# All seven scalings of the last attention pair directly behind its sums, and fewer weight passes in the two drain steps

## The chip, the core and the metric

The kernel runs on one core of a Trainium2 chip. The metric is the device time of one execution in microseconds (us). The core's engines run their own instruction streams and wait for each other through semaphores: TensorE (PE) does the matmuls, VectorE (DVE) and ScalarE (ACT) the elementwise work, SyncE (SP) issues most of the loads and stores.

## The reference

What must be computed is causal attention over 2 batches of 12 heads (448 positions, 64 wide), then two feed-forward layers over the 896 tokens (768 wide, 2048 hidden), all in float32:

```
scores = q @ k.T / 8, masked above the diagonal
attn   = exp(scores - max);  attn = attn / sum(attn)
x      = attn @ v, as 896 x 768
h = relu(x @ w1);  x = (h * h) @ w2
h = x @ w3;        out = (h - tanh(h)) @ w4
```

The weights arrive as float64 words, which the kernel turns into pairs of float32r tiles on the chip.

## The kernel before, in words

**Attention.** Two heads are worked on together as a pair; there are 12 pairs, and `body` runs a loop of 14 steps (`s` = 0 to 13). In step `s`, pair `s` gets its scores, maxima and exponentials (`exps`, L305, on ACT, which also sums each row), pair `p = s - 1` gets its reciprocals (`recips`, L309 and L310) and its scalings by them (`norms`, L317, seven blocks of 64 to 448 columns, numbered 0 to 6, on DVE), and pair `a = s - 2` is transposed (`transposes`, L323, four batches of four on PE), copied out of PSUM (`tcopy`, L329, on ACT) and multiplied with v (`pv`, L341). The result goes to the tiles x as a rounded half (`xhi`, L354, ACT) and a remainder (`xlo`, L358, DVE). The two last steps, 12 and 13, have no new pair: they are called the drains here. In step 12 the last pair (11) is scaled and pair 10 is transposed; in step 13 pair 11 is transposed.

**Early matmuls.** From step 8 on, `fill` puts matmuls of the first layer (batch 0, L370 to L372, three per k) between the attention's PE instructions. They share one PSUM bank, which `relus` (L387, L388, L380 on ACT) empties and whose low half `relu_lows` (L383, DVE) writes.

**Weights.** Each of 64 weight units u (128 x 768 words) is loaded into one of three buffers (`w_load`, L98, SP) and prepared in four passes on DVE: shift (L115), merge (L120), sign (L125) and split (L134 for odd u, L136 for even u). ACT does a scaling of the exponent words (`w_exp`, L105, before merge) and a cast of the word that sign made (L127, before split). The order on DVE is shift(u), split(u-1), merge(u), sign(u), shift(u+1), and so on. Split(u) frees the buffer, and asks for the load of unit u+3.

**What sets the order.** Each engine runs its instructions in the order in which the code issues them. A call of `one` takes the next pass if the budget of the step is above zero (and, for sign, a ring place is free); `pump` takes passes until it isn't. The budget of a drain is `SHARE_LAST`; a pass takes 470 or 870 from it. ACT's share of a pass is put on the list `act_late` and issued by the next `late`.

**After the attention** come the groups of the first layer (8 column blocks m by 2 batches b, 18 matmuls each), then 12 groups of the second (24 matmuls each), and the whole once more for the other half of the hidden columns; then the second feed-forward layer in the same way. Six groups (m = 0 to 5, batch 0) are done early; the first one behind the drains is m = 6, batch 0, with unit 6.

Of the kernel before, what the change touches and what calls it, by code (L numbers as in the profile page):

```python
# [27 lines left out]
NPAIR = B * NP  # L28
# [6 lines left out]


SHARE_PAIR = (800, 3300)
SHARE_LAST = 6000
SHARE_HIDDEN = (2400, 500)
SHARE_OUT = 4000  # L40

# [23 lines left out]
def body(ctx: ExitStack, tc: tile.TileContext, qT, kT, vL, w1, w2, w3, w4, out):  # L65
# [29 lines left out]
    def w_load(u):  # L95
        if u < NU:
            raws[u] = sb.tile([P, UC], I64, tag="raw", bufs=3, name=f"raw{u}")
            nc.sync.dma_start(out=raws[u], in_=units[u])  # L98
# [54 lines left out]
    def room():  # L153
        i = len(taken) - RING
        return i < 0 or taken[i] < freed[0]
# [10 lines left out]
    def late():  # L166
        while act_late:
            act_late.pop(0)()

    def one():  # L170

        if todo and budget[0] > 0 and (room() or not todo[0][3]):
            take()
            return True

    def take():
        f, cost, _, _ = todo.pop(0)
        f()
        budget[0] -= cost
# [6 lines left out]
    def pump():  # L186
        while one():
            pass
# [29 lines left out]
    def warm(count):  # L218
        o = ps.tile([P, 512], F32, tag="h", bufs=1, name="warm")[:, :S]
        for _ in range(count):  # L220
            nc.tensor.matmul(o, lhsT=ones[:, :P], rhs=ones, start=True, stop=True)
# [41 lines left out]
    def scores(n, t):  # L263
        q, k = qk[n]
        banks = []
        for z, cs in enumerate(step(n, t)):
            bank = ps.tile([P, 512], F32, tag="s", bufs=4, name=f"s{n}_{t}_{z}")
            banks.append(bank)
            for c in cs:
                sc[n, c] = bank[:, SOFF[c] : SOFF[c] + D * (c + 1)]  # L270
        for i in range(2):
            for z, cs in enumerate(step(n, t)):
                for c in cs[i : i + 1]:
                    for j in range(2):
                        r, e = slice(D * j, D * j + D), D * (j ^ z)
                        nc.tensor.matmul(sc[n, c][e : e + D], lhsT=q[r, D * c : D * c + D], rhs=k[r, : D * (c + 1)], start=(c == cs[0]), stop=False, skip_group_check=True)  # L276
        for z, cs in enumerate(step(n, t)):
            d = [SOFF[c] // D + c for c in cs]
            o = banks[z].rearrange("p (b k) -> p b k", k=D)[:, d[0] : d[-1] + 1 : max(d[-1] - d[0], 1)]
            for j in range(2):  # L280
                r, e = slice(D * j, D * j + D), D * (j ^ z)
                nc.tensor.matmul(o[e : e + D], lhsT=identb[r, r], rhs=maskb[r, : len(cs)], start=False, stop=True, skip_group_check=True)
        if t == 1:
            qk.pop(n)
            load_qk(n + 3)

    def blocks(n, t):
        return [c for cs in step(n, t) for c in cs]

    def maxes(n, t):  # L290
        if t == 0:
            stat[n] = sb.tile([P, 3, 8], F32, tag="stat", bufs=4, name=f"st{n}")
        st = stat[n]
        cs = blocks(n, t)
        for c in reversed(cs):
            nc.vector.tensor_reduce(out=st[:, 0, SI[c] : SI[c] + 1], in_=sc[n, c], axis=AX.X, op=ALU.max, negate=True)  # L296
        a, z = SI[cs[0]], SI[cs[-1]] + 1
        nc.vector.tensor_scalar_mul(out=st[:, 0, a:z], in0=st[:, 0, a:z], scalar1=0.125)  # L298

    def exps(n, cs):  # L300
        st = stat[n]
        for c in cs:
            w = D * (c + 1)
            i = SI[c]
            nc.scalar.activation(prob[n % 3][:, POFF[c] : POFF[c] + w], sc.pop((n, c)), AF.Exp, bias=st[:, 0, i : i + 1], scale=0.125, accum_out=st[:, 1, i : i + 1])  # L305

    def recips(n):
        st = stat[n]
        nc.vector.tensor_scalar_add(out=st[:, 1, :NQ], in0=st[:, 1, :NQ], scalar1=1e-9)  # L309
        nc.vector.reciprocal(out=st[:, 2, :NQ], in_=st[:, 1, :NQ])  # L310

    def norms(n, cs):
        st = stat[n]
        for c in cs:
            i = SI[c]
            p = prob[n % 3][:, POFF[c] : POFF[c] + D * (c + 1)]
            nc.vector.tensor_scalar_mul(out=p, in0=p, scalar1=st[:, 2, i : i + 1])  # L317

    def transposes(n, t):
        bank = tb[n, t] = ps.tile([P, 512], F32, tag="t", bufs=2, name=f"t{n}_{t}")  # L320
        for i, (kc, c) in enumerate(TBLK[4 * t : 4 * t + 4]):
            o = bank.rearrange("p (i j q) -> p i j q", j=2, q=D)[:, i, :: -1 if c in TURNED else 1]
            nc.tensor.transpose(o, prob[n % 3][:, POFF[c] + P * kc : POFF[c] + P * kc + P], ident)  # L323

    def tcopy(n, t):
        if t == 0:
            pt[n] = slot(3 + n % 2, [P, 16, P], F32, f"pt{n}")
        bank = tb.pop((n, t))
        nc.scalar.copy(out=pt[n][:, 4 * t : 4 * t + 4], in_=bank.rearrange("p (i q) -> p i q", q=P))  # L329

    def pv(n, kcs):
        b, hp = divmod(n, NP)
        if 0 in kcs:
            ob[n] = ps.tile([P, 512], F32, tag="o", bufs=1, name=f"o{n}")
        o = ob[n]
        for kc in kcs:
            r = P if kc < 3 else D
            m = NQ - 2 * kc
            for j in range(2):
                h = 2 * hp + j  # L340
                nc.tensor.matmul(  # L341
                    o[D * j : D * j + D, P * kc : S],
                    lhsT=vs[b][kc][:r, D * h : D * h + D],
                    rhs=pt[n][:r, TBASE[kc] : TBASE[kc] + m, D * j : D * j + D],
                    start=(kc == 0),
                    stop=(kc == 3),
                    skip_group_check=True,
                )
        if 3 in kcs:
            pt.pop(n)  # L350

    def xhi(n):
        b, hp = divmod(n, NP)
        nc.scalar.copy(out=x[hp][:, 0, b], in_=ob[n][:, :S])  # L354

    def xlo(n):
        b, hp = divmod(n, NP)
        nc.vector.tensor_sub(out=x[hp][:, 1, b], in0=ob.pop(n)[:, :S], in1=x[hp][:, 0, b])  # L358
# [117 lines left out]
    def fill(count):  # L476
        for _ in range(count):
            next(early_groups, None)

    def relus():  # L480
        while done:
            h, dst = done.pop(0)
            lows.append((dst, relu2(h, dst)))

    def relu_lows():
        while lows:
            lo_of(*lows.pop(0))
# [34 lines left out]
    for s in range(NPAIR + 2):  # L522
        p, a = s - 1, s - 2
        ss, sp, sa = s < NPAIR, 0 <= p < NPAIR, a >= 0
        f = s - 2 >= NP
        if ss:
            budget[0] = min(budget[0], 0) + (SHARE_PAIR[f] if s > 1 else 0)
            e0, e1 = blocks(s, 0)[::-1], blocks(s, 1)
        else:
            budget[0] = min(budget[0], 0) + SHARE_LAST  # L530
        if sp:
            exps(p, blocks(p, 1)[-1:])
        if ss:
            scores(s, 0)
        if sa:
            norms(a, (3, 5, 6))
        if a >= 1:
            xhi(a - 1)
        if f:
            relu_lows()  # L540
            one()
            fill(1)
        if sa:
            transposes(a, 0)
            tcopy(a, 0)
            transposes(a, 1)
            tcopy(a, 1)
        late()
        if f:
            fill(2)  # L550
        if ss:
            maxes(s, 0)
        if a >= 1:
            xlo(a - 1)
        if f:
            one()
        if ss:
            exps(s, e0[:2])
        if sp:
            recips(p)  # L560
            norms(p, (0, 1, 2))
        if f:
            one()
        if ss:
            scores(s, 1)
        if f:
            fill(1)
        if sa:
            transposes(a, 2)
            tcopy(a, 2)  # L570
            transposes(a, 3)
            tcopy(a, 3)
        if f:
            fill(2)
        late()
        if ss:
            exps(s, e0[2:])
            maxes(s, 1)
            exps(s, e1[:-1])
        if sp:  # L580
            norms(p, (4,))
        relus()
        one()
        if f:
            one()
        if sa:
            pv(a, range(4))
        if not ss:
            pump()
        late()  # L590
        if s == 1:
            warm(5)
        if s in (2, 3):
            w_load(s - 1)
        if s == 4:
            load_v(1)
# [58 lines left out]
```

## Time and profile before

| | before |
|---|---|
| median of 3 runs | 567.02 us |
| lowest of them | 565.03 us |
| profiled execution | 565.34 us |
| its span | 563.5 us |
| PE busy in the span | 551.8 us (98%) |
| DVE busy | 403.8 us (72%) |
| ACT busy | 337.1 us (60%) |
| granted TensorE clock, mean | 0.997 |

The span is the time from the first to the last instruction; 1.84 us of the profiled execution lie around it. A busy PE is one whose pipeline holds a matmul; the duration of one overlaps the next one's, so that start-to-start distances tell the rate. A granted clock of 1.00 is the higher of the two levels (2.4 GHz), 0.50 the lower (1.2 GHz).

### The profile page before, as it was taken

Reading aid. Unit: us, or ns where it says so; the run is one execution under the profiler, and the core shown is the slowest. Engines: PE = TensorE matmul, PEld = TensorE weight load, DVE = VectorE, ACT = ScalarE, POOL = GpSimd, SP = SyncE. Lnnn points to the kernel's source line nnn. Section 1 sums busy time; section 2 is a strip of 40 time slices with the busy share of each in tenths; the row PEclk is TensorE's granted clock in tenths of the full one; section 3 lists DMA queues with packets and bytes.
Section 4 is the critical chain, followed back from the end, with each engine's and each line's share of the span. In section 5 each row is a group of like instructions: output and inputs, shape, how many; then the busy total and the mean of one; then the engine's idle time right before and its main releaser. Section 6 shows DMA issues by size and latency. Waiting matters only on the chain.

```text
span 563.5 us, 8049 instructions
## 1 busy us (share of the span) xinstructions
PE 551.8 (98%) x3134; PEld 482.3 (86%) x3134; DVE 403.8 (72%) x727; ACT 337.1 (60%) x650; POOL 1.8 (0%) x11
## 2 busy tenths in 40 slices
PE   7999999899999999999999999999999999999997
PEld 3667776699999999999999999999999999999996
DVE  5999988658564447555749489998888499889611
ACT  4999888658543238666325278776565487864200
POOL 1000000000000000000000000000000000000000
PEclk9999999899999999999999999999999999999999
DMA  8643412415342324333223330110665311015211
GB/s 292 235 150 106 147 57 82 142 57 168 113 169 94 131 61 163 112 113 112 72 97 116 109 113 1 56 58 15 209 223 176 120 42 56 1 57 173 94 49 49
DMA packets 15525, 61.85 MB, mean 110 GB/s; under 512 B 1664, under 2 KB 6400, under 8 KB 15488
## 3 DMA queue, kind: packets, MB, share of 16 engines
q1 hardware_dynamic: 15200, 61.00, 32.3%
q8 instruction: 24, 0.39, 0.3%
q10 hardware_dynamic: 288, 0.34, 0.2%
q14 instruction: 13, 0.11, 0.1%
HBM read 58.59 MB, written 2.75 MB: 109 GB/s over the span
## 4 chain that ended last, share of the span: by engine, by line
PE 83%; DVE 11%; ACT 2%; DMA 2%; SPq 1%; issue 0%; DVEq 0%; ACTq 0%
PE o L370 14%; PE o L371 14%; PE o L372 14%; PE h L370 13%; PE h L371 13%; PE h L372 13%; DVE st L296 4%; DVE p L317 2%; DMA k<-kT 2%; PE t L323 1%; ACT p L305 1%; DVE raw L120 1%; DVE x L358 1%; PE o L341 1%; DVE w L136 1%; PE s L276 1%
## 5 line engine op out<-in xcount | busy, mean ns | idle before, releaser
L370 PE MATMUL o<-g,w 128*128 128x448 f32 x384 | 140.4, 366 | 0.0
L371 PE MATMUL o<-g,w 128*128 128x448 f32 x384 | 140.4, 366 | 0.0
L372 PE MATMUL o<-g,w 128*128 128x448 f32 x384 | 140.1, 365 | 0.0
L370 PEld LDWEIGHTS o<-g,w 128*128 128x128 f32 x384 | 72.1, 188 | 6.0
L372 PEld LDWEIGHTS o<-g,w 128*128 128x128 f32 x384 | 72.1, 188 | 6.0
L371 PEld LDWEIGHTS o<-g,w 128*128 128x128 f32 x384 | 72.1, 188 | 5.8
L127 ACT CAST w<-raw 128x768 fp32r<-128x768 f32 x64 | 58.3, 911 | 30.6 <-DVE raw L125 30.6
L370 PE MATMUL h<-x,w 128*128 128x448 f32 x192 | 73.2, 381 | 2.4 <-ACT r L387 2.4
L105 ACT ACTIVATE raw<-raw 128x768 f32<-128x768 f32 x64 | 59.4, 928 | 24.4 <-DMA raw<-w 24.4
L371 PE MATMUL h<-x,w 128*128 128x448 f32 x192 | 70.8, 369 | 0.0
L372 PE MATMUL h<-x,w 128*128 128x448 f32 x192 | 70.7, 368 | 0.0
L372 PE MATMUL h<-y,w 128*128 128x448 f32 x192 | 70.6, 368 | 0.0
L371 PE MATMUL h<-y,w 128*128 128x448 f32 x192 | 70.6, 367 | 0.0
L370 PE MATMUL h<-y,w 128*128 128x448 f32 x192 | 70.6, 367 | 0.0
L125 DVE SCALAR_TENSOR_TENSOR raw<-raw 128x768 int32<-128x768 int32 x64 | 61.2, 957 | 1.2
L120 DVE SCALAR_TENSOR_TENSOR raw<-raw 128x768 int32<-128x768 int32 x64 | 61.0, 953 | 0.0
L136 DVE TENSOR_TENSOR w<-raw,w 128x768 fp32r<-128x768 f32 x32 | 30.6, 957 | 31.6 <-ACT w L127 31.5
L305 ACT ACTIVATE p<-s,st 128x128 f32<-128x128 f32 (+6 forms) x84 | 41.2, 530 | 11.1 <-DVE st L298 9.8
L383 DVE TENSOR_TENSOR g<-r,g 128x448 fp32r<-128x448 f32 x32 | 20.0, 625 | 35.7 <-ACT g L380 35.6
L134 DVE SCALAR_TENSOR_TENSOR w<-w,raw 128x768 fp32r<-128x768 f32 x32 | 30.6, 957 | 18.6 <-ACT w L127 18.5
L370 PEld LDWEIGHTS h<-x,w 128*128 128x128 f32 x192 | 36.3, 189 | 6.7 <-ACT r L387 2.8
L372 PEld LDWEIGHTS h<-x,w 128*128 128x128 f32 x192 | 36.2, 189 | 3.4
(57 smaller groups left out, 750.6 us busy)
## 6 DMA issues: line engine op xcount, KB each, us to landing
raw<-w SPq DMA_DIRECT2D x64, 768.0 KB, 4.3
q<-qT SPq DMA_DIRECT2D x12, 224.0 KB, 4.9
k<-kT SPq DMA_DIRECT2D x11, 224.0 KB, 4.1
out<-part SPq DMA_DIRECT2D x11, 224.0 KB, 1.9
v<-vL SPq DMA_DIRECT2D x2, 1152.0 KB, 6.9
vend<-vL SPq DMA_DIRECT2D x1, 384.0 KB, 8.9
k<-kT ACTq DMA_DIRECT2D x1, 224.0 KB, 3.6
out<-part ACTq DMA_DIRECT2D x1, 112.0 KB, 1.7
```

The costliest lines, as they stand in the source:

```text
L105: nc.scalar.activation(h, h, AF.Copy, scale=2.0**-112)
L120: nc.vector.scalar_tensor_tensor(out=lo, in0=hi, scalar=3, in1=lo, op0=ALU.logical_shift_left, op1=ALU.bitwise_or)
L125: nc.vector.scalar_tensor_tensor(out=lo, in0=hi, scalar=-0x80000000, in1=lo, op0=ALU.bitwise_and, op1=ALU.bitwise_or)
L127: act_late.append(lambda: nc.scalar.copy(out=st["w"][:, 0], in_=lo.bitcast(F32)))
L134: nc.vector.scalar_tensor_tensor(out=w[:, 1], in0=w[:, 0].bitcast(F32), scalar=-(1.0 - 2.0**-24), in1=f, op0=ALU.mult, op1=ALU.add)
L136: nc.vector.tensor_sub(out=w[:, 1], in0=f, in1=w[:, 0])
L296: nc.vector.tensor_reduce(out=st[:, 0, SI[c] : SI[c] + 1], in_=sc[n, c], axis=AX.X, op=ALU.max, negate=True)
L305: nc.scalar.activation(prob[n % 3][:, POFF[c] : POFF[c] + w], sc.pop((n, c)), AF.Exp, bias=st[:, 0, i : i + 1], scale=0.125, accum_out=st[ ...
L370: nc.tensor.matmul(h, lhsT=hi, rhs=xh, start=(k == 0), stop=False)
L371: nc.tensor.matmul(h, lhsT=hi, rhs=xl, start=False, stop=False)
L372: nc.tensor.matmul(h, lhsT=lo, rhs=xh, start=False, stop=(k == kk - 1))
L383: nc.vector.tensor_sub(out=dst[1], in0=v, in1=dst[0])
```

## The change

The seven scalings of the last pair, which before were spread over step 12 (blocks 0, 1, 2, then 4) and the start of step 13 (3, 5, 6), are all issued in step 12 directly behind the reciprocals. Two calls of `one` in the drains that stood ahead of this place are taken out (they remain in the steps with a new pair), and the budget of each drain goes from 6000 to 3300.

```diff
-SHARE_LAST = 6000
+SHARE_LAST = 3300
...
-        if sa:
+        if sa and a < NPAIR - 1:
             norms(a, (3, 5, 6))
...
             relu_lows()
-            one()
+            if ss:
+                one()
             fill(1)
...
-        if f:
+        if f and ss:
             one()
...
             recips(p)
-            norms(p, (0, 1, 2))
+            norms(p, (0, 1, 2) if ss else (0, 1, 2, 3, 4, 5, 6))
...
-        if sp:
+        if sp and ss:
             norms(p, (4,))
```

DVE in step 12 before: p_124 is the tile of the last pair's exponentials, x_70 that of pair 9's output, raw_988, raw_1110 and raw_1231 are units 5, 6 and 7.

```order
L115 TENSOR_SCALAR raw_1110<-raw_1110 128x768
L358 TENSOR_TENSOR x_70<-o_1293,x_70 128x448
L134 SCALAR_TENSOR_TENSOR w_1292<-w_1292,raw_988 128x768
L309 TENSOR_SCALAR st_1224<-st_1224 128x7
...
L120 SCALAR_TENSOR_TENSOR raw_1110<-raw_1110 128x768
L317 TENSOR_SCALAR p_124<-p_124,st_1224 128x320
L125 SCALAR_TENSOR_TENSOR raw_1110<-raw_1110 128x768
L115 TENSOR_SCALAR raw_1231<-raw_1231 128x768
L136 TENSOR_TENSOR w_1372<-raw_1110,w_1372 128x768
L120 SCALAR_TENSOR_TENSOR raw_1231<-raw_1231 128x768
L125 SCALAR_TENSOR_TENSOR raw_1231<-raw_1231 128x768
L317 TENSOR_SCALAR p_124<-p_124,st_1224 128x256
```

The same stretch of DVE after the change, from x_70 on:

```order
L358 TENSOR_TENSOR x_70<-o_1293,x_70 128x448
L309 TENSOR_SCALAR st_1224<-st_1224 128x7
...
L317 TENSOR_SCALAR p_124<-p_124,st_1224 128x256
...
L317 TENSOR_SCALAR p_124<-p_124,st_1224 128x448
L115 TENSOR_SCALAR raw_1110<-raw_1110 128x768
L134 SCALAR_TENSOR_TENSOR w_1292<-w_1292,raw_988 128x768
L120 SCALAR_TENSOR_TENSOR raw_1110<-raw_1110 128x768
L125 SCALAR_TENSOR_TENSOR raw_1110<-raw_1110 128x768
L115 TENSOR_SCALAR raw_1231<-raw_1231 128x768
L383 TENSOR_TENSOR g_0_0_2_1309<-r,g_0_0_2_1309 128x448
L358 TENSOR_TENSOR x_71<-o_1373,x_71 128x448
L136 TENSOR_TENSOR w_1383<-raw_1110,w_1383 128x768
```

The reciprocals and all scalings stand ahead of every pass; the split of unit 6 (L136) moves behind the output of pair 10 (x_71).

ACT from the end of step 12 into step 13 after the change (before, raw_1231's L105 stood ahead of step 12's last two copies, and two L127 and one L105 ahead of x_71):

```order
L380 CAST g_0_0_2_1309<-r 128x448
L105 ACTIVATE raw_1231<-raw_1231 128x768
L127 CAST w_1383<-raw_1110 128x768
L354 CAST x_71<-o_1373 128x448
L329 COPY pt_1398<-t_0_1393 128x512
L329 COPY pt_1398<-t_1_1400 128x512
L329 COPY pt_1398<-t_2_1419 128x512
L329 COPY pt_1398<-t_3_1425 128x512
L387 ACTIVATE r<-h_0_1389 128x448
L388 ACTIVATE r<-r 128x448
L380 CAST g_0_0_2_1309<-r 128x448
L105 ACTIVATE raw_1370<-raw_1370 128x768
```

The cast of unit 6 (w_1383) still stands ahead of x_71 and of the four copies of the last pair, and unit 8's L105 (raw_1370) has moved behind them. PE issues the same instructions in the same order as before. From the second group behind the drains on, DVE, ACT and SP do so too.

## Rows read from the trace of the kernel before

**Rows 1.** Waits of PE, whole span: engine, line, releaser; us, times, longest

```profile
PE t L323 <- DVE p L317: 2.6, 1, 2.6
PE h L370 <- ACT r L387: 2.4, 3, 1.4
```

**Rows 2.** Busy time by windows: us, busy per engine, PEclk, DMA share, GB/s

```profile
90.00:92.00 2.00, 0.60 (x9) 0.24 (x5) 2.00 (x5) 1.97 (x8) 0.00 (x0) 1.00 0.18 74
102.00:104.00 2.00, 0.55 (x3) 0.47 (x3) 1.97 (x5) 0.83 (x2) 0.00 (x0) 0.70 0.72 240
104.00:106.00 2.00, 2.00 (x8) 1.73 (x7) 2.00 (x5) 1.80 (x5) 0.00 (x0) 0.50 0.37 154
112.00:562.00 450.00, 448.23 (x2195) 411.65 (x2193) 308.81 (x447) 242.67 (x385) 0.00 (x0) 1.00 0.30 99
```

**Rows 3.** Timeline of PE in the drains: start, us, instruction [idle before, releaser]

```profile
91.96 0.47 PE L370 MATMUL h<-x,w 128*128 128x448 f32 x1 [1.40 <-ACT r L387]
...
92.68 1.03 PE L323 MATMUL t<-ident,p 128*128 128x128 f32 x8
93.47 0.45 PE L370 MATMUL h<-x,w 128*128 128x448 f32 x1
...
95.40 1.04 PE L323 MATMUL t<-ident,p 128*128 128x128 f32 x8
...
100.35 0.49 PE L323 MATMUL t<-ident,p 128*128 128x128 f32 x3
103.45 1.38 PE L323 MATMUL t<-ident,p 128*128 128x128 f32 x5 [2.62 <-DVE p L317]
104.48 0.72 PE L370 MATMUL h<-x,w 128*128 128x448 f32 x1
...
107.20 1.03 PE L323 MATMUL t<-ident,p 128*128 128x128 f32 x8
...
109.39 1.84 PE L341 MATMUL o<-pt,v 128*64 128x448 f32 x12
...
111.42 0.47 PE L370 MATMUL h<-x,w 128*128 128x448 f32 x1
```

**Rows 4.** Timeline of DVE in the drains

```profile
95.28 0.95 DVE L134 SCALAR_TENSOR_TENSOR w<-w,raw 128x768 fp32r<-128x768 f32 x1
96.15 0.16 DVE L309 TENSOR_SCALAR st<-st 128x7 f32<-128x7 f32 x1
...
96.58 0.68 DVE L317 TENSOR_SCALAR p<-p,st 128x64 f32<-128x64 f32 x3
97.18 0.95 DVE L120 SCALAR_TENSOR_TENSOR raw<-raw 128x768 int32<-128x768 int32 x1
98.05 0.38 DVE L317 TENSOR_SCALAR p<-p,st 128x320 f32<-128x320 f32 x1
98.34 0.97 DVE L125 SCALAR_TENSOR_TENSOR raw<-raw 128x768 int32<-128x768 int32 x1
99.23 0.55 DVE L115 TENSOR_SCALAR raw<-raw 128x768 int32<-128x768 int32 x1
100.31 0.96 DVE L136 TENSOR_TENSOR w<-raw,w 128x768 fp32r<-128x768 f32 x1 [0.53 <-ACT w L127]
...
102.17 0.96 DVE L125 SCALAR_TENSOR_TENSOR raw<-raw 128x768 int32<-128x768 int32 x1
103.05 1.04 DVE L317 TENSOR_SCALAR p<-p,st 128x256 f32<-128x256 f32 x3
```

**Rows 5.** Timeline of ACT in the second drain

```profile
100.88 0.92 ACT L105 ACTIVATE raw<-raw 128x768 f32<-128x768 f32 x1 [0.60 <-DMA raw<-w]
103.17 0.91 ACT L127 CAST w<-raw 128x768 fp32r<-128x768 f32 x1 [1.37 <-DVE raw L125]
103.98 0.52 ACT L354 CAST x<-o 128x448 fp32r<-128x448 f32 x1
104.41 1.07 ACT L329 COPY pt<-t 128x512 f32<-128x512 f32 x2
```

## The prediction

> **What bounds the kernel now.** I read the list of PE's waits first, then the busy time by windows, then the timelines of PE, DVE and ACT in the drains. The windows show that PE is the bound: from 112 us to its last matmul it is busy without a gap, 448.23 us of a 450 us stretch that reaches past its end, while DVE is busy for 308.81 us of it and ACT for 242.67 us [rows 2]. The list shows what little PE still waits for. The longest single wait is the one this change is about, 2.6 us of the transposes for the scalings [rows 1].
>
> PE's timeline shows the place. The last pair's first eight transposes begin at 100.35; three run, and the other five come 2.62 us late [rows 3]. DVE's timeline shows why: blocks 3, 5 and 6 begin only at 103.05, behind a shift, a split, a merge and a sign, of which the split itself waited 0.53 us for ACT [rows 4]. None of these passes is wanted soon. A second loss hides behind the first: after the pause the granted clock is 0.50 from 104 to 106 us (the lower level) [rows 2], so the nine matmuls behind the transposes go slowly too.
>
> **The change, part by part.** *The scalings move ahead.* After x of pair 9, DVE is free at 95.28, where split(5) now starts [rows 4]. The reciprocals take 0.43 (96.15 to 96.58), blocks 0 to 2 take 0.60 (96.58 to 97.18), block 4 takes 0.29 (98.05 to 98.34), and the other three at most 1.04 [rows 4]. All scalings are done by 95.28 + 0.43 + 0.60 + 0.29 + 1.04 = 97.64, 2.7 us before the transposes want them. Seven scalings and two reciprocal instructions are issued as before; only their place changes.
>
> *What PE gets back.* Elsewhere in the drain eight transposes take 0.79 to the next matmul (92.68 to 93.47) and nine early matmuls take 1.93 (93.47 to 95.40) [rows 3]. Here the same work takes from 100.35 to 107.20, 6.85 us [rows 3]. The difference is 6.85 - 0.79 - 1.93 = **4.13 us**: 2.62 of pause and 1.51 of lower clock. PE's order is unchanged, so all behind it can start 4.13 us earlier: the second transposes at 103.07, pv at 105.26, the first group behind the drains at 107.29 instead of 111.42 [rows 3].
>
> *The clock term.* It rests on the clock not falling when there is no pause. A pause of 1.40 us at 91.96 [rows 3], in a window where PE was busy 0.60 of 2.00 us, left the granted clock at 1.00 [rows 2], and the matmuls behind it ran at the full pitch used above. That pause stands ahead of the change and stays. The bounds are 0 and 1.51; I take 1.51, since the change leaves no pause in the stretch where the clock fell. The Trainium skill ("TensorE: Matmul & The Clock Gate", section "A second HAM failure mode: psum-queue depth-cycling") speaks against this term: it tells of a kernel whose short idle times between groups of matmuls were enough to make the clock swing between its levels. By that page the remaining 1.40 us pause, with any short new wait, could pull the clock down again, and the gain would be 2.62. The 1.00 behind the 1.40 us pause disagrees with it here.
>
> *The passes move back.* Now they run behind 97.64: shift(6) at most 0.55, split(5) 0.87 (95.28 to 96.15), merge(6) 0.95, and sign(6), whose result ACT casts 1.00 after sign's start (102.17 to 103.17) [rows 4, 5]. That puts ACT's cast of unit 6 at 97.64 + 0.55 + 0.87 + 0.95 + 1.00 = 101.01. This wait is new in its place: behind the cast in ACT's queue stand x of pair 10 and the first copies of the last pair. The cast takes 0.81 to the next start, x 0.43, the two copies 1.07 together [rows 5]: the copies begin at 102.25 and end at about 102.79 and 103.32. PE wants these banks back for the second transposes at 103.07 and, four transposes (half of 0.79) later, 103.47. So the copies are hidden by nine matmuls, with 0.28 and 0.15 us to spare. My sum uses whole durations where pieces overlap, so the true margin should be a little larger. I take 0 here; the upper bound is below, in the rivals.
>
> *The smaller budget.* 3300 a drain lets five passes run in each; merge(8) and split(7) slip behind the drains. Split(6) ends before at 100.31 + 0.96 = 101.27, and unit 6 is wanted at 111.42: 10 us of cover [rows 3, 4]. After the change it follows x of pair 10 on DVE: ACT's part of that x ends at 101.01 + 0.81 + 0.52 = 102.34 [rows 5], DVE's part is bounded by a pass (0.95) and split(6) takes 0.96 [rows 4], so it ends at about 104.25, for a PE that now comes at 107.29. Cover of 3.0 us is left. Unit 7 is wanted only after eight further groups and units 8 and up after ten; a group is 18 matmuls, twice the nine that take 1.93 [rows 3], so these are some 30 us away, and the passes meet the old order again in the second group. Cost 0.
>
> *The loads.* Split(5) frees the buffer of unit 8. Before, it ended at 96.15, and ACT's L105 got the unit at 100.88, 4.73 later [rows 4, 5]. Now it ends at 97.64 + 0.55 + 0.87 = 99.06, and the load lands by 103.8. ACT's L105 for it has moved behind the last pair's four copies and the relus, which wait for PE's last early matmul just ahead of pv at 105.26. So it lands in time. The loads of units 9 and 10 are asked for later as well, and are wanted later still. SP does nothing else there. Cost 0.
>
> **Sum.** 565.34 (the profiled execution: span 563.5 and 1.84 around it) - 4.13 = 561.21. The runs shown are 565.03 at the lowest and 567.02 as the median, so the profiled one lies near the lower end; from the middle of the two, 566.0, I get **561.9**.
>
> **Rivals.** (a) *The copies come late.* If DVE's five passes take longer than in the rows, ACT's cast slips, and with it the copies; each microsecond beyond 0.15 becomes a wait of PE at the second transposes. For it: the margin is thin, and ACT really waits there. Against it: each piece has a row. With 1.0 us of slip PE loses 0.85, and the time is 562.8. (b) *The clock still falls*, as the page has it: 566.0 - 2.62 = 563.4. For it: the drain keeps a pause of 1.40. Against: the clock stood at 1.00 behind that one. (c) *Slower: the prepared unit 6 becomes the late one.* The place is the first group behind the drains, which needs split(6). The cover falls from 10 to 3.0 us; later than that, each microsecond stops PE. It decides from 3.0 us of lateness, and from 3.0 + 4.13 = 7.1 us the kernel is slower than before; to lose 2% (11.3 us) it would be 18 us late. A stuck ring of DVE waiting for ACT's x behind ACT's cast behind DVE's sign could do it; but the waits of this kind in the rows are 0.53 and 1.37 us [rows 4, 5]. (d) *PE gains elsewhere too*, because the waits for the relus (2.4 us in all [rows 1]) shrink: the longest stands ahead of the change, so at most 1 us, and 560.9.
>
> **Chances.** The forecast 0.78, (a) 0.12, (b) 0.05, (c) 0.02, (d) 0.03. The range takes the forecast from the lower run, 565.03 - 4.13 = 560.9, less the 1 us of (d): 560.0. At the top stands (b) from the higher run with a little of (a): 567.02 - 2.62 + 0.6 = 565.0. Two per cent, about what a measurement of this kernel can tell from no change, are 11.3 us; all waits in rows 1 with the slow clock are 2.6 + 2.4 + 1.51 = 6.5 us, so faster by more has 0.01, slower by more 0.01 (the far end of (c)), and within it 0.98.
>
> **What would show it.** Right: no wait of the transposes for the scalings in PE's list; a granted clock of 1.00 throughout the drains; 0.79 and 1.93 between the last pair's transposes; the last pair's seven scalings in one row on DVE ending near 97.6; the first group behind the drains about 15.3 us after the matmul at 91.96 instead of 19.46. Wrong: a wait of the second transposes for ACT's L329 (a), a window at 0.50 (b), a wait of L370 for L134 or L136 (c), or any wait of PE behind the drains.

## The result, and the profile after

The changed kernel takes 561.86 us in the median of 20 runs (lowest 561.12), against 566.77 us for the kernel before in its 20 runs (one of which took 1904.64 us; without it the median is 566.75). The ratio is 0.9917, with a 95% interval of 0.9902 to 0.9931: 0.8% faster, clear of the noise and well inside 2%. The profiled execution took 561.35 us with a span of 559.5, 4.0 us less than the span before.

The longest of PE's waits after the change (engine, line, releaser; us, times, longest):

```profile
PE h L370 <- ACT r L387: 2.4, 3, 1.4
PE s L276 <- ACT p L305: 2.0, 2, 1.8
PE s L276 <- DMA k<-kT: 1.1, 2, 0.6
...
```

The wait of the transposes for the scalings [rows 1] is gone, nothing in the drains took its place, and the waits for the relus are what they were. The windows of the changed kernel, in the columns of rows 2:

```profile
90.00:92.00 2.00, 0.70 (x10) 0.28 (x6) 2.00 (x6) 1.86 (x7) 0.00 (x0) 1.00 0.23 95
102.00:104.00 2.00, 2.00 (x16) 1.85 (x14) 1.57 (x4) 1.55 (x4) 0.00 (x0) 1.00 0.36 151
104.00:106.00 2.00, 2.00 (x13) 1.37 (x13) 1.97 (x3) 1.41 (x3) 0.00 (x0) 1.00 0.42 95
112.00:558.00 446.00, 444.23 (x2176) 408.20 (x2174) 307.81 (x446) 242.82 (x384) 0.00 (x0) 1.00 0.31 102
```

PE is busy for the whole of 102 to 106, where it was busy for 0.55 of the first 2 us and slow in the next [rows 2]; the granted clock stays at 1.00. Behind the drains nothing is late: 444.23 us busy up to the last matmul. PE's timeline of the same stretch as rows 3:

```profile
92.10 0.48 PE L370 MATMUL h<-x,w 128*128 128x448 f32 x1 [1.40 <-ACT r L387]
...
100.29 0.36 PE L372 MATMUL h<-x,w 128*128 128x448 f32 x1
100.49 1.04 PE L323 MATMUL t<-ident,p 128*128 128x128 f32 x8
101.28 0.45 PE L370 MATMUL h<-x,w 128*128 128x448 f32 x1
...
103.21 1.03 PE L323 MATMUL t<-ident,p 128*128 128x128 f32 x8
...
105.40 1.84 PE L341 MATMUL o<-pt,v 128*64 128x448 f32 x12
...
107.43 0.47 PE L370 MATMUL h<-x,w 128*128 128x448 f32 x1
```

From the pause of 1.40, which stayed, to the first group behind the drains it now takes 107.43 - 92.10 = 15.33 us, against 111.42 - 91.96 = 19.46 before [rows 3]: 4.13 us less. All eight transposes run in one piece, 0.79 to the next matmul, and the nine matmuls take 1.93. DVE and ACT of the changed kernel in that stretch:

```profile
94.88 0.62 DVE L358 TENSOR_TENSOR x<-o,x 128x448 fp32r<-128x448 f32 x1 [0.97 <-ACT x L354]
95.42 0.16 DVE L309 TENSOR_SCALAR st<-st 128x7 f32<-128x7 f32 x1
...
95.86 1.93 DVE L317 TENSOR_SCALAR p<-p,st 128x64 f32<-128x64 f32 x7
97.70 0.55 DVE L115 TENSOR_SCALAR raw<-raw 128x768 int32<-128x768 int32 x1
98.17 0.97 DVE L134 SCALAR_TENSOR_TENSOR w<-w,raw 128x768 fp32r<-128x768 f32 x1
...
102.99 0.95 DVE L136 TENSOR_TENSOR w<-raw,w 128x768 fp32r<-128x768 f32 x1
```

```profile
101.05 0.93 ACT L127 CAST w<-raw 128x768 fp32r<-128x768 f32 x1 [0.60 <-DVE raw L125]
101.86 0.55 ACT L354 CAST x<-o 128x448 fp32r<-128x448 f32 x1
102.29 1.10 ACT L329 COPY pt<-t 128x512 f32<-128x512 f32 x2
...
107.17 0.89 ACT L105 ACTIVATE raw<-raw 128x768 f32<-128x768 f32 x1
```

The seven scalings are one row and end near 97.7. ACT waits 0.60 us for sign(6) ahead of the cast at 101.05, the new wait that was forecast, and the two copies end at about 102.84 and 103.39. PE wants them at 103.21 and 103.61: 0.37 and 0.22 us to spare. Unit 8 was there when ACT came to it at 107.17.

### The profile page after: what moved, and what is told of

Same layout as the page of the kernel before. It is cut to its first block, busy times and chain, and to the rows that moved or that the text cites. A ratio compares the mean times of both kernels' runs of the same rounds, so it can differ in the third digit from the quotient of the medians.

```text
span 559.5 us, 8048 instructions
## 1 busy us (share of the span) xinstructions
PE 549.9 (98%) x3134; PEld 481.6 (86%) x3134; DVE 403.9 (72%) x727; ACT 336.7 (60%) x650; POOL 1.8 (0%) x11
## 4 chain that ended last, share of the span: by engine, by line
PE 84%; DVE 11%; ACT 2%; DMA 2%; SPq 1%; issue 0%; DVEq 0%; ACTq 0%
PE o L370 14%; PE o L371 14%; PE o L372 14%; PE h L370 13%; PE h L371 13%; PE h L372 13%; DVE st L296 4%; DVE p L317 2%; DMA k<-kT 2%; PE o L341 1%; PE t L323 1%; ACT p L305 1%; DVE x L358 1%; DVE raw L120 1%; DVE st L298 1%; PE s L276 1%
## 5 line engine op out<-in xcount | busy, mean ns | idle before, releaser
L127 ACT CAST w<-raw 128x768 fp32r<-128x768 f32 x64 | 58.1, 908 | 30.5 <-DVE raw L125 30.4
L105 ACT ACTIVATE raw<-raw 128x768 f32<-128x768 f32 x64 | 59.3, 927 | 22.5 <-DMA raw<-w 22.5
L136 DVE TENSOR_TENSOR w<-raw,w 128x768 fp32r<-128x768 f32 x32 | 30.6, 957 | 31.1 <-ACT w L127 31.0
L370 PEld LDWEIGHTS h<-x,w 128*128 128x128 f32 x192 | 36.1, 188 | 6.7 <-ACT r L387 2.8
L370 PEld LDWEIGHTS h<-y,w 128*128 128x128 f32 x192 | 36.0, 188 | 3.4
```

Source lines behind the costliest of these rows:

```text
L105: nc.scalar.activation(h, h, AF.Copy, scale=2.0**-112)
L127: act_late.append(lambda: nc.scalar.copy(out=st["w"][:, 0], in_=lo.bitcast(F32)))
L136: nc.vector.tensor_sub(out=w[:, 1], in0=f, in1=w[:, 0])
L370: nc.tensor.matmul(h, lhsT=hi, rhs=xh, start=(k == 0), stop=False)
```

## The experiments

**The parts of the change.** The first three kernels do one part of it or leave one out.

Scalings only, on the kernel before:

```diff
-        if sa:
+        if sa and a < NPAIR - 1:
             norms(a, (3, 5, 6))
...
-            norms(p, (0, 1, 2))
+            norms(p, (0, 1, 2) if ss else (0, 1, 2, 3, 4, 5, 6))
...
-        if sp:
+        if sp and ss:
             norms(p, (4,))
```

> Before, with all seven scalings of the last pair behind the reciprocals, and nothing else of the change. Theory A (both parts are needed: with a budget of 6000 a second cast of weights and unit 8's L105 stand on ACT ahead of the last pair's copies): the wait for the scalings is gone, but the second transposes wait for ACT's L329. From the rows of before, sign(7) would start near 103.2, its cast near 104.2, x of pair 10 near 105.0, the first copy end near 106.0, against transposes that want it at 103.1: about 2.9 us of pause, and 1.5 us of lower clock if the clock falls. Time 565 to 566.5, about that of before. Rival B (late scalings were the whole cause): 561 to 562.5 and no wait of the transposes.

Measured: 566.29 us against 566.48 for the kernel before on the same chip, ratio 1.0004 (0.9989 to 1.0020). No gain. PE and then ACT in the second drain of this kernel:

```profile
100.93 1.04 PE L323 MATMUL t<-ident,p 128*128 128x128 f32 x8
...
106.72 1.20 PE L323 MATMUL t<-ident,p 128*128 128x128 f32 x8 [2.91 <-ACT pt L329]
...
108.09 0.57 PE L371 MATMUL h<-x,w 128*128 128x448 f32 x1
108.47 0.57 PE L372 MATMUL h<-x,w 128*128 128x448 f32 x1
108.84 0.57 PE L370 MATMUL h<-x,w 128*128 128x448 f32 x1
```

```profile
101.03 0.91 ACT L127 CAST w<-raw 128x768 fp32r<-128x768 f32 x1 [0.98 <-DVE raw L125]
101.84 0.92 ACT L105 ACTIVATE raw<-raw 128x768 f32<-128x768 f32 x1
104.83 0.92 ACT L127 CAST w<-raw 128x768 fp32r<-128x768 f32 x1 [2.06 <-DVE raw L125]
105.65 0.53 ACT L354 CAST x<-o 128x448 fp32r<-128x448 f32 x1
106.07 1.08 ACT L329 COPY pt<-t 128x512 f32<-128x512 f32 x2
```

The windows, in the columns of rows 2:

```profile
108.00:110.00 2.00, 2.00 (x6) 1.38 (x5) 0.57 (x1) 1.12 (x3) 0.00 (x0) 0.50 0.58 190
```

The first transposes now run in one piece, but the pause has moved to the second ones, and is about as long as before (2.91 us, 2.62 before): the passes of the large budget put a second cast (104.83) on ACT ahead of the copies. Behind the pause the matmuls start 0.37 to 0.38 us apart instead of about 0.20, at a granted clock of 0.50: the lower clock came back too. Theory A holds and its 2.9 us were right.

Fewer passes only, with the scalings where they were:

```diff
-SHARE_LAST = 6000
+SHARE_LAST = 3300
...
             relu_lows()
-            one()
+            if ss:
+                one()
...
-        if f:
+        if f and ss:
             one()
```

> Before, with the two calls of one taken out of the drains and the budget at 3300; the scalings stay where they were. Theory A (what made the scalings late was the passes ahead of them, and five passes in place of eight are few enough): blocks 3, 5 and 6 are scaled from about 100.2 to 101.2, and the transposes that begin at 100.35 wait at most 0.5 us for them; the granted clock stays at 1.00; 561.5 to 562.5, within 0.6 us of the changed kernel. Rival B (the place directly behind the sums is what counts): the wait for the scalings stays above 1.5 us and the time above 564.

Measured: 562.04 us, ratio 0.9927 (0.9914 to 0.9939), whose interval overlaps that of the whole change. No wait of the transposes for the scalings stands in PE's list. What the late scalings still cost is seen in PE's timeline:

```profile
100.38 1.48 PE L323 MATMUL t<-ident,p 128*128 128x128 f32 x8
101.61 0.45 PE L370 MATMUL h<-x,w 128*128 128x448 f32 x1
```

The eight transposes take 1.23 us to the next matmul instead of 0.79, so they were held up for 0.44 us in all. Moving the scalings is worth that much, in this trace, once the passes are fewer; the medians do not tell the two kernels apart.

The changed kernel with the budget of before:

```diff
-SHARE_LAST = 3300
+SHARE_LAST = 6000
```

> The changed kernel with the drains' budget back at 6000. Theory A: ACT gets unit 8's L105 (whose load is asked for near 99 and lands near 103.7) and a second cast ahead of the last pair's copies; the copies start near 106 and the second transposes wait about 3.6 us for them, with 1.5 us of lower clock: 565.5 to 567.5, no faster than before. Rival B (the budget only matters for the passes ahead of the scalings, and here they are behind them): 561 to 562.5.

Measured: 566.63 us, ratio 1.0011 (0.9998 to 1.0025). PE and ACT of this kernel:

```profile
107.17 1.97 PE L323 MATMUL t<-ident,p 128*128 128x128 f32 x8 [3.31 <-ACT pt L329]
```

```profile
104.02 0.92 ACT L105 ACTIVATE raw<-raw 128x768 f32<-128x768 f32 x1 [1.59 <-DMA raw<-w]
105.32 0.89 ACT L127 CAST w<-raw 128x768 fp32r<-128x768 f32 x1 [0.38 <-DVE raw L125]
```

Unit 8's L105 and the second cast stand ahead of the copies, PE waits 3.3 us for these, and the granted clock is 0.50 from 106 to 112 us (in an execution of 567.86 us, 1.2 above the median). So the budget is the part that the gain hangs on; the place of the scalings without it gains nothing, nor do the two calls of `one` taken out. The smaller budget with those two calls left in was not run, so whether it is enough by itself is not shown.

**Where the budget begins to hurt.** Two budgets between:

```diff
-SHARE_LAST = 3300
+SHARE_LAST = 4200
```

> The changed kernel with a budget of 4200 in the drains: one pass more, split(6), in the first drain, and in the second one ACT's L105 of unit 8 between the last pair's two pairs of copies. The first copies keep their place on ACT, so by the theory of the thin cover the second transposes wait for nothing; the later copies may come 0.7 us later, ahead of pv, which has 0.5 us to spare: 561.5 to 562.5, clock 1.00. Rival (each pass more costs its time): 562.5 to 563.

Measured: 561.33 us, ratio 0.9914 (0.9897 to 0.9930), a little under the expected range. The traced execution is one of two long ones of the six (564.00 us, with a late k at its start), but PE waits for nothing in its drains: from the pause of 1.40 to the first group behind them it takes 15.33 us, as in the changed kernel. The sixth pass is free.

```diff
-SHARE_LAST = 3300
+SHARE_LAST = 5100
```

> The changed kernel with a budget of 5100: merge(7) comes into the first drain too, and with it ACT's L105 of unit 8 ahead of x of pair 10 and the last pair's first copies. That unit's load is asked for near 99 and lands near 103.7, so the copies start near 105 and the second transposes wait about 2.4 us for them, mostly with the lower clock behind: 564.5 to 566. It tells the two blocks of the budget of 6000 apart, the load and the second cast: if the second cast alone held the copies there, this one stays below 563.

Measured: 563.94 us, ratio 0.9964 (0.9953 to 0.9975), a little under the expected range. ACT of this kernel:

```profile
101.11 0.92 ACT L127 CAST w<-raw 128x768 fp32r<-128x768 f32 x1 [0.62 <-DVE raw L125]
103.55 0.92 ACT L105 ACTIVATE raw<-raw 128x768 f32<-128x768 f32 x1 [1.52 <-DMA raw<-w]
...
104.78 1.07 ACT L329 COPY pt<-t 128x512 f32<-128x512 f32 x2
```

The seventh pass puts unit 8's L105 ahead of the copies, ACT waits 1.52 us for its load, and PE waits 1.99 us for the copies. The load alone is enough to hold them. The clock stayed at 1.00 in this trace. Five of the seven runs have a mean granted clock of 1.00 and took 563.6 to 564.2 us, under the range; two have 0.997 and took 564.9, inside it.

**The thin cover.** Two, then six, subtractions on DVE behind the last pair's scalings:

```diff
             norms(p, (0, 1, 2) if ss else (0, 1, 2, 3, 4, 5, 6))
+            if not ss:
+                junk = tmp("junk", "w")
+                for _ in range(2):
+                    nc.vector.tensor_sub(out=junk, in0=prob[p % 3][:, :S], in1=prob[p % 3][:, :S])
```

The changed kernel ran once more as their base:

> The changed kernel once more, beside the next three on the same chip: 561.2 to 562.5, as before; it is the base for the differences of the others.

Measured: 561.70 us, ratio 0.9918 (0.9904 to 0.9931).

> The changed kernel with two subtractions (128x448, into a tile that nobody reads) on DVE behind the last pair's scalings, ahead of shift(6): all passes of the drain slip by about 1.08 us (2 x 0.54, the pitch of L383 in the trace), and with them ACT's cast, x of pair 10 and the last pair's first copies. Theory of the thin cover (the copies have 0.37 and 0.22 us to spare in the trace of the changed kernel): the second transposes lose 1.08 - 0.22 = 0.86 us, clock at 1.00; 0.7 to 1.1 us above the changed kernel. Rival (the cover is wider than it looks, since something else than the copies holds the transposes): less than 0.3 us above it.

Measured: 562.48 us, 0.78 above the base. DVE and PE of this kernel:

```profile
97.82 1.27 DVE L566 TENSOR_TENSOR junk<-p 128x448 f32<-128x448 f32 x2
...
99.48 0.95 DVE L134 SCALAR_TENSOR_TENSOR w<-w,raw 128x768 fp32r<-128x768 f32 x1
```

```profile
100.49 0.47 PE L372 MATMUL h<-x,w 128*128 128x448 f32 x1
...
101.59 0.45 PE L370 MATMUL h<-x,w 128*128 128x448 f32 x1
...
104.24 1.14 PE L323 MATMUL t<-ident,p 128*128 128x128 f32 x8 [0.56 <-ACT pt L329]
105.14 0.45 PE L370 MATMUL h<-x,w 128*128 128x448 f32 x1
```

The nine matmuls and the wait take 2.65 us instead of 1.93, the transposes 0.90 instead of 0.79: 0.83 us lost, where 0.86 were expected. The copies are the next thing that holds PE, and their cover is as thin as the rows said. The agreement has two errors in it. The two subtractions hold DVE for 1.19 us (97.82 to the next shift at 99.01), not 1.08. And split(5), which now ends at 100.43, is late for the third early matmul of the second drain (100.49), so that the first transposes start 0.92 us after the first of these matmuls instead of 0.72. The whole stretch from the pause of 1.40 to the first group behind the drains is 16.37 us, 1.04 more than in the changed kernel's trace, where the medians differ by 0.78.

The same with `range(6)`:

> The same with six subtractions: a slip of about 3.24 us. Thin cover: a pause of 2.9 us ahead of the second transposes, 3.0 us lost. Clock theory (a pause of this size costs the lower clock behind it, whatever PE waits for): a window at 0.50 and 1 to 2 us more: 4 to 5 us above the changed kernel, about the time of the kernel before. Rival (the lower clock of the kernel before came from something else in that stretch): the clock stays at 1.00 and only 3.0 us are lost.

Measured: 565.84 us, 4.1 above the base, in the range that was expected, but not by the way that was expected. DVE and PE of this kernel:

```profile
105.70 0.95 DVE L134 SCALAR_TENSOR_TENSOR w<-w,raw 128x768 fp32r<-128x768 f32 x1
```

```profile
103.78 0.36 PE L371 MATMUL h<-x,w 128*128 128x448 f32 x1
106.70 0.47 PE L372 MATMUL h<-x,w 128*128 128x448 f32 x1 [2.57 <-DVE w L134]
107.01 1.04 PE L323 MATMUL t<-ident,p 128*128 128x128 f32 x8
...
110.46 1.14 PE L323 MATMUL t<-ident,p 128*128 128x128 f32 x8 [0.56 <-ACT pt L329]
```

The long wait is not at the second transposes. It stands ahead of the first ones, for split(5): the early matmuls of the second drain use unit 5, and its low half is wanted by the third of them. The six subtractions hold DVE for 3.83 us (101.40 to 105.23), not 3.24, and split(5) ends at 106.65. The copies then cost 0.56 once more. From the pause of 1.40 to the first group behind the drains it takes 19.01 us, 3.68 more than in the changed kernel, and in this trace the clock stayed at 1.00 from 90 to 112 us. So a pause of this size does not always cost the lower clock, and the clock theory in the form "any pause of this size" is refuted. But the trace is of the longest of the ten executions (568.73 us), with a late k and the lower clock at 16 to 20 us. Of the other nine, seven have a mean granted clock of 0.997 and two of 0.999, and all took 565.6 to 566.0. Whether the clock fell in the drains of those seven no trace shows.

**A further wait of PE.** The changed kernel with the relus ahead of the second maxima:

```diff
             exps(s, e0[2:])
+            relus()
             maxes(s, 1)
             exps(s, e1[:-1])
```

> The changed kernel with the relus of an early group (L387, L388, L380) ahead of the second maxima and their exponentials instead of behind them, so that ACT empties the bank of the early matmuls 1.7 us earlier, in a time in which it waits for DVE's maxima (1.31 us). Theory A (PE's waits for the relus, 2.4 us in three, are lost time like the pause that the change removed): these waits vanish, the exponentials start about 0.4 us later without PE noticing; 559.3 to 560.7. Rival B (the pair's chain through ACT is what sets the pace of these steps, so the delay of the exponentials comes back as a wait of the scores or transposes): 561.5 to 563. A side question: whether executions with a mean granted clock of 0.994, 2 of 20 of the changed kernel and about 4 us longer, vanish with the pause of 1.40 us.

Measured: 558.33 us, ratio 0.9874 (0.9853 to 0.9895). This beats both kernels, by more than theory A had expected. The profiled execution was the one long one of six, 562.29 us; its trace shows a wait of 3.2 us for the third pair's k near the start and a granted clock of 0.91 in the first 20 us. So a longer execution can come without the pause of 1.40, which this kernel lacks; the two long ones of the changed kernel have no trace.

> The changed kernel with the early relus once more: 558.0 to 558.8, and, in an execution whose first loads are not late, no wait of PE in the steps with early matmuls; against the changed kernel the steps 9 to 11 take 9.65 us each instead of 9.9, 10.1 and 10.3.

Measured: 558.37 us, ratio 0.9865 (0.985 to 0.988). The pv of steps 8 to 11 and of step 13 in PE's timeline:

```profile
57.91 1.84 PE L341 MATMUL o<-pt,v 128*64 128x448 f32 x12
...
67.56 1.84 PE L341 MATMUL o<-pt,v 128*64 128x448 f32 x12
...
77.21 1.84 PE L341 MATMUL o<-pt,v 128*64 128x448 f32 x12
...
86.85 1.84 PE L341 MATMUL o<-pt,v 128*64 128x448 f32 x12
...
102.18 1.84 PE L341 MATMUL o<-pt,v 128*64 128x448 f32 x12
```

The steps with a new pair and early matmuls take 9.65 us each. From the first early matmul (51.12 here, 51.53 in the changed kernel) to the last pair's pv it takes 51.06 us, against 105.40 - 51.53 = 53.87: 2.81 us gained in these steps. The list of waits had named 2.4 of them; the remaining 0.4 are stretched steps that it does not name. The medians of the two kernels (561.70 and 558.37 us, on different chips) differ by 3.3 us, of which 0.41 lie ahead of the early matmuls in these two traces; that part was not followed up.

The same edit on the kernel before:

> The kernel before, with only the relus moved ahead of the second maxima, and nothing of the change. If the two gains are independent (different waits of PE, in different steps), it keeps the wait of the transposes for the scalings with the lower clock behind it, loses the waits for the relus, and gains what that edit gained on the changed kernel, 3.0 to 3.7 us: 562.7 to 563.5. Rival (the gain of the early relus came out of the drains): the gain here is under 2 us.

Measured: 563.25 us, ratio 0.9948 (0.9936 to 0.9961), 2.8 us less than the kernel before on the same chip (566.08), a little under the 3.0 to 3.7 expected; its wait of the transposes for the scalings is still there, 2.7 us, with the granted clock at 0.50 from 102 to 104 us. The two gains are of different waits. On this chip they are 4.4 us (the changed kernel once more) and 2.8 us, 7.2 together; both edits together gave 8.1 us on two other chips. They add up to within about 1 us, and what makes the rest is not shown.

## Why the prediction was right, point by point

- *PE is the bound, and the pause with its lower clock is what the change gets back.* Right: 4.13 us in the drain, as forecast. That the time agrees as well, 561.9 forecast and 561.86 measured, is in part luck. The forecast started from 566.0, the middle of the two ordinary runs of three (the third is the one of 1904.64 us), and 20 runs have their median at 566.77; so the medians differ by 4.91 us, where the two traced executions differ by 3.99. The 0.8 us beyond 4.13 stand in no row of these traces. The two errors, in the start and in the gain, cancel.
- *The scalings end by 97.64, far ahead of the transposes.* Right (near 97.7). But the forecast gave this move the whole gain, and the runs show a different share: alone it gained nothing, and the fewer passes without it gained all but about 0.4 us (as read from its trace). The 2.62 us pause was the time of the passes ahead of the scalings, and there were two ways of taking them out of the way. Only the fewer passes kept the pause from coming back at the next link. The forecast came out right because it priced the whole change as it stood.
- *The smaller budget, cost 0.* Right as a price, and too short as a reading. It was costed as work put off, for what it might make late. It is also what keeps ACT's queue clear ahead of the last pair's copies: with 6000 the pause came back there with 3.3 us.
- *The copies hidden with 0.28 and 0.15 us to spare.* Right: 0.37 and 0.22, the difference being the whole durations in the sum. Rival (a) was the right one to fear; 1.19 us of slip cost 0.78 by the medians, of which the copies are the larger part in the trace.
- *The clock term.* 1.51 us came back in full. As a rule it was too simple: the lower clock stands behind the 2.62, 2.91 and 3.31 us pauses, and in the traces not behind 1.40, not behind 1.99 with seven passes, and not behind 2.57 with the slip. The Trainium skill's section on depth-cycling ("TensorE: Matmul & The Clock Gate", "A second HAM failure mode: psum-queue depth-cycling"), by which short idle times would be enough to make the clock swing, does not show here: the 1.40 us pause stayed, and no window from 90 to 112 us fell below 1.00. Rival (b) did not happen.
- *The cover of unit 6.* Right in size: split(6) ended at 103.94 for a PE that came at 107.43, 3.5 us of cover where 3.0 were forecast (and 4.0 to the group's third matmul, the first that reads what split writes). But the forecast looked at the wrong unit for rival (c): unit 5 is wanted first, in the second drain, and its split ended at 99.14 for a matmul at 100.29. The cover of 1.15 us was not in the working, and it is what the slip of 3.83 us ran into; 1.19 us already touched it.
- *The loads, and (d).* Right that the loads cost nothing, and no gain came from the relus by itself; that took an edit of its own.

## What to carry to other kernels

When a pause is filled by work that somebody put ahead of what is waited for, read both queues that this work feeds: taking the waiting step to the front of one engine (DVE) only moved the pause here, because the same passes stood in the other engine's queue (ACT) ahead of the next link. Before costing put-off work at nothing, list every unit that it delays in the order in which it is wanted; the first one, not the most conspicuous one, has the least cover. And a pause on the bounding engine is to be priced with the matmuls behind it, from start to start, but the part of the lower clock is not a fixed price.

## What the runs showed of the hardware that was not expected

The lower clock behind a pause of PE is not decided by the length of that one pause: behind 2.62 and 2.91 us rows at 0.50 follow, behind 2.57 us with another place in the program the clock stayed at 1.00 in the one trace of it. In ten runs of the scalings alone, two kept a mean granted clock of 0.999 to 1.0 and took 565.0 to 565.1 us, and seven others with 0.997 took 565.8 to 566.6: about 1.2 us for it, if it is this stretch in which they differ, which no trace of the two shows (the tenth, with 0.991, took 570.3). With seven passes it is the same picture: two of seven runs at 0.997 took about 1 us longer than the five at 1.00. What decides it stays open. The lower clock also stands behind a late load of the third pair's k: with 3.2 us of waiting (the early relus), 2.8 us (six subtractions) and 2.4 us (the budget of 4200) the granted clock was 0.91 to 0.92 over the first 20 us, and these executions were about 3 to 4 us longer than most others of their kernels. In the trace of the scalings alone, a wait of 1.6 us there left it at 1.00.
